# Banks of a score set on Trainium2: a third bank from anywhere, read by a second exponential, and a new rule string for the planner

## The chip, the cores and the metric

The kernel runs on one core of a Trainium2 chip. The metric is device time in microseconds (us) of one execution. The core's engines run side by side, each through its own list of instructions: TensorE (PE in the profile, its weight loads PEld), VectorE (DVE), ScalarE (ACT), GpSimd (POOL), and SyncE (SP), which issues most DMAs. PSUM, where TensorE writes, has eight banks of 512 fp32 columns by 128 partitions.

## The reference

One layer: attention with 32 query heads and one key and value head of width 20, beside a feed-forward block, both on the normalised input, added to it.

```python
xn = _layernorm(x)                        # x: 1 x 2048 x 640, bf16
q = (xn @ wq).reshape(B, S, 32, 20).transpose(0, 2, 1, 3)
k = xn @ wk                               # 2048 x 20
v = xn @ wv
p = softmax(einsum("bhqd,bkd->bhqk", q, k) * 20 ** -0.5)
o = einsum("bhqk,bkd->bhqd", p, v)
return x + o.transpose(0, 2, 1, 3).reshape(B, S, 640) @ wo + silu(xn @ w1) @ w2   # w1: 640 x 1728
```

## The kernel before

**The work.** Four blocks of 512 queries (QC) by eight groups of four heads (NG) make 32 groups; each has 16 tiles of 128 keys. One item is the scores of one head, one key tile and one block: a matmul of 32 rows by 128 columns of the array with 512 columns streamed (line 1078), into one PSUM bank. There are 32 x 16 x 4 = 2048 items. The four heads of a group lie on four row groups of the array, so up to four scores of different heads run side by side as one round.

**Two ways to the exponential.** An item is taken either by ScalarE, which reads two or three neighbouring banks with one Exp (line 1166) into slots of `Ebuf`, or by VectorE, which turns a whole batch of four items (one group, one key tile) into three integer approximations: a first step per item (line 1409, `p1`), then two shifts of the four together, on POOL (line 1448) or VectorE (line 1453). ScalarE takes key tiles from the front of a group, VectorE claims them from its back (`claim`). The products with V (line 1201) are column matmuls, four side by side as one round of 128 x 32 tiles, into the bank U of the group: one round for a key tile that ScalarE did, three for one that VectorE did. U is copied out by VectorE (line 1250), or added to what an earlier part left (line 1249).

**The other work** fills TensorE in between: projections to q (job "q"), the feed-forward's first product ("h", with a tanh on ScalarE at line 773 and its VectorE step at line 776), the second with the output projection ("out", VectorE at line 903), and for the last block "y" (line 919) and "fin" (line 967). These are column matmuls recorded by the helper `col_mm` (line 447); where a score run leaves a row group free, a slice of 32 rows can stand in it (`row_mm`, line 454). After each group its sums of weights go through DMAs and a reciprocal (lines 848 to 856) to POOL's product (line 860), and DMAs pack the result (line 873). If TensorE would have nothing to do for a while, a matmul of zeros is put in (`filler`, line 1725).

**What sets the order.** A planner, which runs on the host while the program is built, writes all five lists. It keeps a clock for each engine (`Sched`), always takes the engine whose clock is furthest back, and gives it the best of the operations at hand by a list of preferences. On TensorE these are: scores for ScalarE (`make_s_act`), scores for VectorE, products with V, and the other jobs. `plan(n)` picks the banks of ScalarE's n-th set from those that are free: the earliest three neighbouring banks if they come in time, else two. `act_until` says until when ScalarE has work, from its clock and the exponentials made but not begun. A set is made only when exponential n-2 has been committed.

The choices hang on some thirty numbers (`BASE`), and a letter stands for a variant of a few of them (`RULES`). `PLAN` is a string with one letter for each 10 us of the planner's TensorE clock; at each such step the numbers are set to `BASE` and the letter's variant. So a letter in the string changes the whole order from its place on. `split` and `spat`, which the change adds, are such numbers too.

Switching TensorE between row tiles (scores) and column tiles (the rest) costs a turn, so the planner gathers runs of each.

## Time and profile before

| | |
|---|---|
| median of 3 runs | 691.98 us (691.73 to 692.18) |
| the profiled execution | 691.7 us, its span 689.9 us |
| granted TensorE clock | 1.000 |
| instructions of the trace | 22614 |
| first exponential starts, last one ends | 13.35 us, 673.35 us |
| exponentials (line 1166) | 654: 590 of two banks, 64 of three |
| items by ScalarE / by VectorE | 1372 / 676 |
| matmul records at lines 1078, 1201, 447 | 2048, 3400, 3792 |

The profile's page gives busy time by engine, the span in 40 slices, the chain of work that ended last, and groups of instructions by line. In a row of a group stand the line, engine, operation, what is written and read, the shapes and the count; then the busy time in us and the mean duration in ns; then the idle time of the engine before these instructions, and what ended it. Timeline rows begin with the start and the length of a stretch in us. Rows of waits give the total in us, how often, and the longest. "Busy" counts a moment once however many instructions of the engine overlap in it.

The span has three parts: 13 us of loads and normalisation until the first exponential, the attention stage, and 16.6 us after the last exponential, in which the last groups' products and sums and the last output tiles are made.

### The profile page before, as it was taken

What the parts mean: (1) busy time and instruction counts of PE and PEld (TensorE: products, weight loads), DVE (VectorE), ACT (ScalarE), POOL (GpSimd) and SP (SyncE); (2) the same over time, 40 slices, a digit from 0 to 9 for tenths busy, and PEclk for the clock granted to TensorE, in tenths of its full rate; (3) what the DMA queues carried; (4) which work ended last, traced back from release to release, by engine and by line L of the source; (5) the groups of instructions that cost most, each with busy time, mean ns of one, the idle gap of its engine ahead of it and who ended that gap; (6) DMA issues with size and microseconds to landing.
All of it is one profiled execution on the core that took longest, in us unless ns stands there. A gap on an engine that the chain in (4) does not pass through costs nothing.

```text
span 689.9 us, 22614 instructions
## 1 busy us (share of the span) xinstructions
PE 676.4 (98%) x9870; PEld 234.4 (34%) x9873; DVE 594.7 (86%) x1017; ACT 665.9 (97%) x726; POOL 583.9 (85%) x351
## 2 busy tenths in 40 slices
PE   8999999999999999999999999999999999999998
PEld 5432222322233333323233333322232333333345
DVE  7899989988998867898988888798988889989973
ACT  6999999999999999999999999999999999999990
POOL 6668899898988889898899899989889998888860
PEclk9999999999999999999999999999999999999999
DMA  7753221122221232321212223222222202223201
GB/s 217 178 180 42 20 20 15 33 35 30 18 28 12 31 40 30 69 34 17 33 14 30 29 31 40 23 65 29 29 19 22 22 18 32 31 23 68 23 7 41
DMA packets 34241, 28.97 MB, mean 42 GB/s; under 512 B 15486, under 2 KB 29662, under 8 KB 34142
## 3 DMA queue, kind: packets, MB, share of 16 engines
q1 hardware_dynamic: 33854, 27.20, 25.7%
q8 instruction: 77, 1.26, 0.8%
q10 hardware_dynamic: 288, 0.33, 0.1%
q14 instruction: 22, 0.18, 0.1%
HBM read 11.09 MB, written 2.62 MB: 20 GB/s over the span
## 4 chain that ended last, share of the span: by engine, by line
PE 76%; ACT 16%; DVE 4%; POOL 1%; SPq 1%; DMA 1%; issue 1%; DVEq 0%; ACTq 0%
PE psall L1201 26%; PE psall L1078 25%; PE psall L447 23%; ACT sbt L1166 14%; DVE sbt L1409 1%; ACT sbt L773 1%; POOL sbt L1448 1%; SPq L706 1%; DMA sbt<-sbt 0%; PE psall L621 0%; DVE sbt L563 0%; PE psall L734 0%; DVE sbt L607 0%; PE psall L1725 0%; DVE sbt L565 0%
## 5 line engine op out<-in xcount | busy, mean ns | idle before, releaser
L1166 ACT ACTIVATE sbt<-psall 128x1024 bf16<-128x1024 f32 (+1 forms) x654 | 643.0, 1156 | 2.3 <-PE psall L1078 2.1
L1448 POOL TENSOR_SCALAR sbt<-sbt 128x2048 int16<-128x2048 int16 x275 | 521.7, 1897 | 70.4 <-DVE sbt L1453 22.4
L1409 DVE TENSOR_SCALAR sbt<-psall 128x512 int16<-128x512 f32 x676 | 441.8, 685 | 64.4 <-PE psall L1078 60.1
L1078 PE MATMUL psall<-sbt 32*128 32x512 bf16 x2048 | 269.2, 384 | 4.3 <-ACT sbt L1166 1.6
L1201 PE MATMUL psall<-sbt 128*32 128x512 bf16 x3400 | 264.8, 384 | 0.6 <-POOL sbt L1448 0.4
L447 PE MATMUL psall<-sbt 128*32 128x320 bf16 (+3 forms) x3792 | 227.6, 332 | 2.5 <-DVE sbt L1409 0.8
L1078 PEld LDWEIGHTS psall<-sbt 32*128 32x128 bf16 x2048 | 71.4, 91 | 238.8 <-ACT sbt L1166 172.7
L447 PEld LDWEIGHTS psall<-sbt 128*32 128x32 bf16 (+1 forms) x3792 | 82.4, 95 | 82.7 <-issue 44.7
L1201 PEld LDWEIGHTS psall<-sbt 128*32 128x32 bf16 x3400 | 70.1, 94 | 114.5 <-issue 71.0
L1453 DVE TENSOR_SCALAR sbt<-sbt 128x2048 int16<-128x2048 int16 x63 | 48.6, 784 | 0.7 <-PE psall L1201 0.6
L860 POOL TENSOR_TENSOR sbt<-sbt 128x512 bf16<-128x512 f32 x30 | 38.2, 1274 | 7.2 <-DVE sbt L1453 5.5
L776 DVE SCALAR_TENSOR_TENSOR sbt<-sbt,psall 128x512 bf16<-128x512 bf16 x52 | 35.6, 684 | 5.2 <-ACT sbt L773 2.6
L773 ACT ACTIVATE sbt<-psall 128x512 bf16<-128x512 f32 x52 | 37.6, 723 | 0.1
L1250 DVE COPY sbt<-psall 128x512 f32<-128x512 f32 x31 | 21.2, 683 | 1.1 <-PE psall L1201 1.0
L454 PE MATMUL psall<-sbt 32*128 32x320 bf16 x70 | 21.3, 305 | 0.0
L1725 PE MATMUL psall<-sbt 128*32 128x256 bf16 (+1 forms) x228 | 14.4, 355 | 1.2 <-DVE sbt L487 1.2
L693 DVE TENSOR_SCALAR sbt<-psall 128x512 bf16<-128x512 f32 x20 | 13.6, 680 | 0.4 <-PE psall L447 0.4
L903 DVE SCALAR_TENSOR_TENSOR sbt<-psall,sbt 128x320 bf16<-128x320 f32 x24 | 11.6, 485 | 2.1 <-PE psall L447 1.6
L572 POOL TENSOR_TENSOR sbt<-sbt 128x2 f32<-128x2 f32 x8 | 5.7, 709 | 8.7 <-DVE sbt L570 8.3
L585 POOL TENSOR_SCALAR sbt<-sbt 128x640 bf16<-128x640 bf16 x12 | 10.4, 874 | 1.5 <-DVE sbt L577 1.5
L919 DVE SCALAR_TENSOR_TENSOR sbt<-psall,sbt 128x320 f32<-128x320 f32 x8 | 3.9, 486 | 8.0 <-PE psall L447 8.0
L1725 PEld LDWEIGHTS psall<-sbt 128*32 128x32 bf16 x228 | 7.0, 114 | 4.5 <-issue 1.6
(64 smaller groups left out, 117.9 us busy)
## 6 DMA issues: line engine op xcount, KB each, us to landing
sbt<-sbt SPq DMA_DIRECT2D x120, 64.0 KB, 3.9
sbt<-in_A_x_dram SPq DMA_DIRECT2D x28, 160.0 KB, 4.0
sbt<-sbt SPq DMA_DIRECT2D x213, 20.0 KB
out_dram<-sbt SPq DMA_DIRECT2D x14, 160.0 KB, 2.0
sbt<-in_B_w_dram SPq DMA_DIRECT2D x1, 2160.0 KB, 13.4
sbt<-in_B_w_dram SPq DMA_DIRECT2D x1, 2080.0 KB, 8.1
sbt<-sbt SPq DMA_DIRECT2D x75, 8.0 KB
sbt<-in_A_wq_dram SPq DMA_DIRECT2D x1, 800.0 KB, 5.9
```

Of the source, the lines that this page charges most:

```text
L447: ins = pe.matmul(ps[j * SLOT:(j + 1) * SLOT, b * BANK + off:b * BANK + off + n], w[:, j * SLOT:(j + 1) * SLOT], x, start=start, stop=stop ...
L454: return pe.matmul(ps[0:w.shape[-1], b * BANK:b * BANK + n], w[k], x[k], start=start, stop=stop, tile_position=(r * SLOT, 0))
L773: t = Op("act", lambda a: a.activation(t_buf[0:rows, ts, :], bk(job.bank, 0, QW, rows=rows), AF.Tanh, scale=0.5), t_act(512), ACT_END, pre ...
L776: u = Op("dve", lambda v: v.scalar_tensor_tensor(out=hT[par][0:rows, fk, :], in0=t_buf[0:rows, ts, :], scalar=1.0, in1=bk(job.bank, 0, QW, ...
L860: nm = pool(lambda e: e.tensor_tensor(oU[:, us, :], U_sb[:, us, :], Rrep, ALU.mult), 1356.0, POOL_END, pre=[uc] + lc + pack_op.get(divmod( ...
L1078: return pe.matmul(bk(b), kT_rep[i * SLOT:(i + 1) * SLOT, kt * P:(kt + 1) * P], qT[i * SLOT:(i + 1) * SLOT, g % NQ, :], start=True, stop=T ...
L1166: return a.activation(Ebuf[:, es * QW:es * QW + w], ps[:, buf[0] * BANK:buf[0] * BANK + w], AF.Exp, scale=ESCALE)
L1201: ins = pe.matmul(ps[i * SLOT:(i + 1) * SLOT, ub * BANK:ub * BANK + QW], lhsT, rhs, start=(first and k < HG), stop=(last and k >= len(lst) ...
L1409: p1 = Op("dve", lambda v: v.tensor_scalar(z16[:, i * QW:(i + 1) * QW], bk(job.bank), ZBIAS, 0.0, ALU.add, ALU.max), t_dve(QW) + 2.0, DVE_ ...
L1448: op = pool(lambda v, t=t, j=j, zin=zin: v.tensor_scalar(t.bitcast(I16), zin, float(SHIFT[j]), 1.0, ALU.add, ALU.mult), POOL_SHIFT, POOL_E ...
L1453: op = dve(lambda v, t=t, j=j, zin=zin: v.tensor_scalar_add(t.bitcast(I16), zin, float(SHIFT[j])), t_dve(N, 4), prio=SPRIO - 0.01 * j, **args)
L1725: ins = pe.matmul(ps[i * SLOT:(i + 1) * SLOT, ub * BANK:ub * BANK + n], zero_t[:, 0:SLOT], zero_t[:, 0:n], start=fresh, stop=fresh, tile_p ...
```

## The change

A set for ScalarE is now a list of runs of neighbouring banks instead of one run. `plan` may return two neighbouring banks and one bank elsewhere (when `split` is 1 or 2), or three neighbouring banks as two and one (`split` 2); then `com` makes two exponentials, of two banks and of one, with successive numbers, and each frees its own banks. `exp_of` is the old body of `com` that makes one exponential. `act_until` looks back over four exponentials instead of two. Four letters are added, R, S, T and U, and `PLAN` is another string: it has the letters R, S and T at seven of its places. `split` is 0 under all other letters.

```diff
-BASE = dict(uopen=4, umin=3, ...)
+BASE = dict(split=0, spat=0.0, uopen=4, umin=3, ...)
...
+             R=dict(split=1), S=dict(split=2), T=dict(split=1, slack=500.0), U=dict(split=2, hungry=2000.0), ...
-PLAN = "acbtJKazNvhaJvxvixrrnrKzDDnQDmoqvknpfLBGvDPmoJdftFQdkttaQBBoknQEaoz"
+PLAN = "aaatJKazNvhaJvxoRozLfTDtJwDTQroaEBzSQaBkBkJvBvzQQttcrcBoTGSEaaatHBzR"
...
     def act_until(n):
-        return sc.t["act"] + sum(exp_ops[i].occ for i in (n - 2, n - 1) if i >= 0 and not exp_ops[i].done)
+        return sc.t["act"] + sum(exp_ops[i].occ for i in range(max(0, n - 4), n) if not exp_ops[i].done)
...
+            c2 = c if k == 2 else c2
         if w[3] is not None and (w[3][0] <= need + ru.patience or w[2][0] >= w[3][0]):
             s, r = w[3]
             if sc.t["dve"] < s + ru.dwant and not any(at[b] <= s + 40.0 for b in at if b not in r) and dve_items() is not None:
-                return r[:2]
-            return r
+                return [r[:2]]
+            return [r[:2], r[2:]] if ru.split >= 2 else [r]
+        if ru.split in (1, 2) and w[2] is not None:
+            c = [(max(s, at[b]), r, b) for s, r in c2 for b in at if b not in r]
+            if c:
+                s, r, b = min(c, key=lambda x: (x[0], -left_over(at, x[1] + (x[2],))))
+                if s <= need + ru.spat and not (sc.t["dve"] < s + ru.dwant and not any(at[x] <= s + 40.0 for x in at if x not in r and x != b) and dve_items() is not None):
+                    return [r, (b,)]
         if w[2] is None or w[2][0] < need - ru.hold:
             return None
-        return w[2][1]
+        return [w[2][1]]
...
+    def exp_of(s_op, n, run, es):
+        k = len(run)
+        for q in range(es, es + k):
+            e_owner[q] = n
+        eo = act(lambda a: a.activation(Ebuf[:, es * QW:(es + k) * QW], ps[:, run[0] * BANK:(run[0] + k) * BANK], AF.Exp, scale=ESCALE),
+                 t_act(k * QW) - 1.0, pre=[s_op], reads=[sc.banks[b] for b in run], writes=[res("E", es + q) for q in range(k)], prio=0.0, name=f"exp{n}")
+        eo.on_commit = lambda op: sc.free.update(run)
+        exp_ops[n] = eo
+        e_users[n] = []
...
-            eo = act(ef, t_act(w) - 1.0, pre=[op], reads=[sc.banks[b] for b in buf], writes=[res("E", es + k) for k in range(len(buf))], prio=0.0,
-                     name=f"exp{n}")
-            eo.on_commit = lambda op: sc.free.update(buf)
+            for run in runs:
+                exp_of(op, n, run, es + at)
+                for j in range(at, at + len(run)):
+                    mine[j] = n
+                at += len(run)
+                n += 1
+                att["n"] += 1
             for j, (g, kt, i) in enumerate(items):
                 d = pv_pend.setdefault((g, kt), {})
-                d[i] = (es + j, eo, n)
+                d[i] = (es + j, exp_ops[mine[j]], mine[j])
```

In the changed kernel the lines behind the new function lie ten further down (1201 is 1211, 1409 is 1419), and the exponential is line 1138.

More of the change, by code (lines that the diff above doesn't have):

```diff
@@ L103 @@
 TRACT = (0, 1)
-BASE = dict(uopen=4, umin=3, uleft=3, uwait=500.0, pace=-1.0, lagl=3, half=6, hold2=0, bnd=4, pj=6000.0, rows=0, rowmin=3, lagmax=6, lagp=0, lagj=6, openlag=5, late=-0.02, lead=0.01, leadmax=0.02, need=640.0, hold=300.0, dwant=600.0, slack=700.0, dnow=400.0, hungry=0.0, patience=0.0, keep=460.0, open=2, zcap=9, stay=0.0, homes=1, want=1, claim=6)
+BASE = dict(split=0, spat=0.0, uopen=4, umin=3, uleft=3, uwait=500.0, pace=-1.0, lagl=3, half=6, hold2=0, bnd=4, pj=6000.0, rows=0, rowmin=3, lagmax=6, lagp=0, lagj=6, openlag=5, late=-0.02, lead=0.01, leadmax=0.02, need=640.0, hold=300.0, dwant=600.0, slack=700.0, dnow=400.0, hungry=0.0, patience=0.0, keep=460.0, open=2, zcap=9, stay=0.0, homes=1, want=1, claim=6)
@@ L109 @@
-PLAN = "acbtJKazNvhaJvxvixrrnrKzDDnQDmoqvknpfLBGvDPmoJdftFQdkttaQBBoknQEaoz"
+             m=dict(need=740.0), n=dict(hold=0.0), o=dict(stay=640.0), p=dict(open=1), q=dict(slack=560.0), r=dict(hungry=1000.0), s=dict(claim=9), t=dict(open=3), u=dict(claim=4), v=dict(want=2), w=dict(slack=850.0), x=dict(hold2=4), y=dict(bnd=0), z=dict(pj=-1e9), A=dict(rows=0), B=dict(rows=2, rowmin=2), C=dict(pj=2000.0), D=dict(openlag=3), E=dict(pj=8000.0), F=dict(hold2=3), G=dict(rows=1), H=dict(half=0), I=dict(half=3), J=dict(stay=560.0), K=dict(stay=720.0), P=dict(need=560.0), Q=dict(hold=120.0), R=dict(split=1), S=dict(split=2), T=dict(split=1, slack=500.0), U=dict(split=2, hungry=2000.0), L=dict(uopen=3), M=dict(uopen=4), N=dict(uopen=5), O=dict(uopen=0))
@@ L1129, in make_s_act @@
             return None
-        buf = plan(n)
-        if buf is None:
+        runs = plan(n)
+        if runs is None:
             return None
+        buf = tuple(b for r in runs for b in r)
         items = next_items(len(buf), peek=True)
@@ L1136, in make_s_act @@
         buf = buf[:len(items)]
+        runs = [x for x in (tuple(b for b in r if b in buf) for r in runs) if x]
         pre = s_pre(items)
@@ L1182, in com @@
                         e_users[nn] = [o for o in e_users[nn] if o is not None] + [po]
-                else:
-                    pass
             for j, (g, kt, i) in enumerate(items):
-                d = pv_pend[(g, kt)]
-                if len(d) < HG and None not in e_users[n]:
-                    e_users[n].append(None)
+                if len(pv_pend[(g, kt)]) < HG and None not in e_users[mine[j]]:
+                    e_users[mine[j]].append(None)
             att["items"] += len(items)
```

19 lines of the change are left out of this document (4 added, 15 removed).

## The prediction

> **What bounds the kernel now.** I read the page's busy line first, then the groups by line and shape, then the stage between the first and the last exponential by itself, and last the timeline of ScalarE and TensorE inside it.
>
> ```profile
> PE 676.4 (98%) x9870; PEld 234.4 (34%) x9873; DVE 594.7 (86%) x1017; ACT 665.9 (97%) x726; POOL 583.9 (85%) x351
> ```
>
> ```profile
> L1166 ACT ACTIVATE sbt<-psall 128x1024 bf16<-128x1024 f32 x590 | 563.9, 1118 | 2.3 <-PE psall L1078 2.1
> L1166 ACT ACTIVATE sbt<-psall 128x1536 bf16<-128x1536 f32 x64 | 95.1, 1509 | 0.0
> L773 ACT ACTIVATE sbt<-psall 128x512 bf16<-128x512 f32 x52 | 37.6, 723 | 0.1
> L631 ACT ACTIVATE sbt<-psall 128x512 bf16<-128x512 f32 x3 | 2.0, 650 | 0.0
> ```
>
> ```profile
> 13.35:673.35 660.00, 652.44 (x9323) 216.54 (x9326) 578.73 (x973) 657.58 (x713) 575.67 (x328) 1.00 0.26 39
> ```
>
> The last row is the attention stage, 660.0 of the 689.9 us; its columns are length, then busy time (count) of PE, PEld, DVE, ACT and POOL, then clock. ScalarE (ACT) looks full, 657.58 us, and so does TensorE (PE), 652.44. Both are too high, because instructions overlap. The pitch, start to start, is what one really costs, and the timeline has it:
>
> ```profile
> 326.20 0.66 ACT L773 ACTIVATE sbt<-psall 128x512 bf16<-128x512 f32 x1
> 326.68 4.77 ACT L1166 ACTIVATE sbt<-psall 128x1024 bf16<-128x1024 f32 x5
> 331.19 0.74 ACT L773 ACTIVATE sbt<-psall 128x512 bf16<-128x512 f32 x1
> ```
>
> ```profile
> 664.06 9.52 ACT L1166 ACTIVATE sbt<-psall 128x1536 bf16<-128x1536 f32 x7
> ```
>
> ```profile
> 668.07 4.17 ACT L1166 ACTIVATE sbt<-psall 128x1536 bf16<-128x1536 f32 x3
> ```
>
> One bank (512) takes 326.68 - 326.20 = 0.48 us, two banks (331.19 - 326.68) / 5 = 0.902. The seven three-bank ones begin at 664.06 and the fifth to seventh, taken alone, begin at 668.07: (668.07 - 664.06) / 3 = 1.337. The smallest pitches of the trace are 0.477, 0.903 and 1.330. So a bank costs 0.427 us and every instruction 0.050 on top. Charged at these, ScalarE's stage is 590 x 0.903 + 64 x 1.330 + 57 x 0.477 (52 tanh, 2 more of line 744 and 3 of line 631) + 0.16 for one small copy = 645.5 us. Against the 660.0 that leaves **14.5 us of waits**, most of them hidden in pitches over the smallest. ScalarE is 97.8% loaded.
>
> TensorE the same way, where a run is a stretch of matmuls of one tile shape:
>
> ```profile
> 304.20 0.39 PE L1078 MATMUL psall<-sbt 32*128 32x512 bf16 x3
> 304.52 0.83 PE L447 MATMUL psall<-sbt 128*32 128x512 bf16 x12
> 305.29 0.39 PE L1078 MATMUL psall<-sbt 32*128 32x512 bf16 x3
> 305.61 0.62 PE L447 MATMUL psall<-sbt 128*32 128x512 bf16 x8
> 306.16 0.39 PE L1078 MATMUL psall<-sbt 32*128 32x512 bf16 x3
> ```
>
> ```profile
> 674.48 2.89 PE L447 MATMUL psall<-sbt 128*32 128x320 bf16 x80
> 677.29 1.05 PE L999 MATMUL psall<-sbt 128*128 128x4 f32 x8
> ```
>
> Twelve column matmuls (three rounds of four) take 0.77 us, eight take 0.55: 0.216 a round and 0.115 for the turn to the next shape. A run of scores takes 0.32: one round and 0.104 for its turn, whether it holds two, three or four. Rounds 320 wide cost (2.81 - 0.10) / 20 = 0.136. Summed over the program's 649 score runs, 643 column runs and 28 others this is 650.1 us, 628.2 of it from the first score to the last, or 95% of the stage. So ScalarE is the tighter of the two, TensorE the next, and VectorE (578.73 of 660, 88%) only follows:
>
> ```profile
> PEld psall L1078 <- ACT sbt L1166: 172.7, 479, 0.8
> DVE sbt L1409 <- PE psall L1078: 60.1, 170, 1.4
> ```
>
> Scores wait 479 times for a bank that an exponential leaves, which is the sign of ScalarE as the bound, and VectorE waits for scores.
>
> By the Trainium skill, "Perfetto Trace Analysis", section Identifying the Most-Contended Engine, matmul occupancy is no measure of the distance from the limit and the weight loads' share is to be taken instead, while ScalarE's occupancy may stand. The page's 34% for PEld agrees that 98% is not TensorE at its limit.
>
> **The change, part by part.** Both kernels' orders are fixed when they are built, so the instructions can be counted in both.
>
> *The planner's code.* The older planner's steps are unchanged while `split` is 0. The sum over four older exponentials instead of two adds nothing then, since exponential n-2 must be committed before a set is made. An exponential that reads neighbouring banks is the same instruction. I charge this nothing: it is work of the host.
>
> *The order.* It is the same on ScalarE up to about 154 us of charged work, and another one from there on. Only eight sets are split in the whole program (at about 154, 205, 262, 264, 340, 341, 568 and 572 us of ScalarE's charged work); a ninth one-bank exponential is the leftover at the end. So the two-and-one set does little by itself: three-bank scores were 64 and are 55 + 8 = 63. What moves time is the new string.
>
> *ScalarE.* Two-bank exponentials go from 590 to 601, three-bank from 64 to 55, one-bank from 0 to 9: 665 for 654, and 1376 banks for 1372. Sum: 11 x 0.903 - 9 x 1.330 + 9 x 0.477 = **+2.3 us**, of it 4 banks x 0.427 = 1.7 and 11 x 0.050 = 0.55. No cover hides this: it is on the tightest engine, unless its 14.5 us of waits shrink.
>
> The Trainium skill, "ScalarE: Activation LUTs", section What ACT_TABLE_LOAD costs, gives 186 ns and 0.833 ns an element, less about 93 ns where two follow each other, so 93 ns for each further instruction where the pitches above give 50. By it the sum would be 4 x 0.427 + 11 x 0.093 = 2.7 us, an estimate; it speaks against splitting.
>
> *VectorE and GpSimd (POOL).*
>
> ```profile
> L1409 DVE TENSOR_SCALAR sbt<-psall 128x512 int16<-128x512 f32 x676 | 441.8, 685 | 64.4 <-PE psall L1078 60.1
> L1453 DVE TENSOR_SCALAR sbt<-sbt 128x2048 int16<-128x2048 int16 x63 | 48.6, 784 | 0.7 <-PE psall L1201 0.6
> L1249 DVE TENSOR_TENSOR sbt<-psall,sbt 128x512 f32<-128x512 f32 x6 | 4.1, 682 | 0.0
> L1448 POOL TENSOR_SCALAR sbt<-sbt 128x2048 int16<-128x2048 int16 x275 | 521.7, 1897 | 70.4 <-DVE sbt L1453 22.4 <-PE psall L1201 16.1 <-DVE sbt L1409 6.2
> ```
>
> First steps 676 to 672, shifts 63 to 62, partial sums of U 6 to 9: -4 x 0.653 - 0.77 + 3 x 0.68 = -1.3 us. POOL has one shift less, -1.9. Both have slack, so by itself this is worth nothing.
>
> *TensorE.* One batch less on VectorE turns three products with V into one: 3400 matmuls become 3392. Fills of 512 columns go from 16 to 13 and those of 256 from 41 to 42, ten more slices of the other products slip into score runs, and runs go to 650, 645 and 27. By the pitches above the sum is 649.1, **-1.0 us**. A fill is issued where the planner sees a hole on TensorE: three holes fewer.
>
> *DMAs.*
>
> ```profile
> PE 76%; ACT 16%; DVE 4%; POOL 1%; SPq 1%; DMA 1%; issue 1%; DVEq 0%; ACTq 0%
> ```
>
> ```profile
> 375.63 3.41 DMA sbt<-sbt
> ```
>
> The same transfers stand in another order on SP's queue. DMAs are 1% of the chain of work that ended last, and the longest piece there took 3.41 us; that one percent is what hides them at present, so I charge nothing. If one came late, a job of products would be held back, by 3.4 us at most.
>
> *What the waits become.* This is the disputed term: the trace of before cannot show it. Bounds: ScalarE's waits stay at 14.5 us (the sum is +2.3), or they fall by what the other engines' progress tells. That can be counted: put both orders side by side at equal charged work of ScalarE, and ask what the others have been given by then.
>
> | ScalarE's charged work, us | scores issued, before / after | TensorE's charged work, before / after |
> |---|---|---|
> | 370 | 1137 / 1131 | 363.0 / 359.7 |
> | 470 | 1458 / 1453 | 459.6 / 456.8 |
> | 570 | 1785 / 1777 | 558.3 / 554.5 |
> | 620 | 1953 / 1947 | 607.5 / 604.2 |
> | 649 | 2042 / 2037 | 633.7 / 631.9 |
>
> From 370 on TensorE has done 3.0 us less and VectorE some six scores less (ScalarE's own count is equal within one). If TensorE stays as full as it was (95.4%), 3.0 / 0.954 = 3.1 us less have passed; if VectorE keeps its rate, 6 x 0.653 / 0.877 = 4.5 us less. ScalarE would then have waited 3.1 to 4.5 us less, and with its 2.3 us more work the sum is -0.9 to -2.2. I take the middle, **-1.5 us**, because fewer fills say that TensorE's holes did not grow. After the last score both programs have 13.4 us of TensorE work left, so the tail adds nothing.
>
> The profiled execution took 691.7 us (its span of 689.9 and 1.8 around it), so the sum is 691.7 - 1.5 = 690.2 for it. The median of the runs, 691.98, lies 0.28 higher; on its scale the forecast is 690.4 after rounding down from 690.5.
>
> **The rivals.**
>
> *The added load counts in full; slower.* ScalarE's 11 further exponentials and four further banks, from 154 us of charged work to the end, cost 2.3 us, and the other engines' smaller progress is simply idleness: their scores wait longer for banks. For it: ScalarE is the tightest, its visible idle before exponentials is 2.3 us only, and three-bank sets, the cheapest per bank, are nine fewer. I also charged TensorE against ScalarE over stretches of four exponentials: what TensorE has in excess adds up to 9.9 us in both orders, so the new one is no smoother. Against: three fills fewer. It decides from the point where ScalarE's waits stay above 12.2 us. Time 691.98 + 2.3 = 694.3. [...]
>
> *The changes cancel; within 0.2%.* ScalarE +2.3, TensorE -1.0, VectorE -1.3: three engines that wait for each other in turn, each keeping its idle time on the average, give a sum of zero. Eight split sets in 665 then show nothing. Time 692.0.
>
> *The split saves a whole run at each place.* Had each of the eight sets saved a score run (0.32 us) ahead of a starved ScalarE, that would be 2.6 us beside the forecast, 690.4 - 2.6 = 687.8. Against: the number of score runs rises by one.
>
> **How the numbers follow.** A measurement of this kernel can tell about 0.2%, 1.38 us: faster is below 690.6, slower above 693.4. Chances: forecast 0.40 and the saved runs 0.02, which together are faster, 0.42; cancelling 0.25; full load 0.33. The forecast is the likeliest. Since cases of both signs hold much of the chance, its own range is 688.6 to 691.2; the range of all reaches from 688.6, where ScalarE's waits have fallen by 5.7 us (the 4.5 of VectorE's reading and four of the eight saved runs, 1.3), to 694.4, the full load; a late DMA and the whole split saving are left out.
>
> **What would show it.** Right: ScalarE's charged work is 647.7 us in the stage, its waits 10 to 12, the stage some 1.5 us shorter, the tail unchanged. Wrong: the waits stay near 14.5 and scores wait as long or longer for exponentials; or new waits stand at the eight one-bank exponentials; or a DMA appears in the chain of waits. The stage until 154 us of charged work should be the same within 0.2 us.

## The result, and the profile after

The changed kernel takes 695.1 us in the median of four executions, the kernel before 691.9 beside it: ratio 1.0049, 95% interval [1.0037, 1.0061]. Two of the four ran at a granted clock of 1.000 (694.4 and 694.5 us) and two at 0.997 (695.7 and 696.0). Five further executions, all at 0.999 or 1.000, gave 694.6 and a ratio of 1.0039 [1.0027, 1.0052] (experiment e5). I therefore take the change as **+2.8 us**; where a difference of 1 us matters below, I compare medians of executions at 0.999 or more. The forecast was 690.4, range 688.6 to 694.4: wrong in its sign, and the result lies above the range.

The page of the changed kernel, its span and first and fourth part:

```profile
span 692.5 us, 22605 instructions
...
PE 677.0 (98%) x9855; PEld 235.9 (34%) x9855; DVE 589.3 (85%) x1015; ACT 667.3 (96%) x737; POOL 582.8 (84%) x350
...
ACT 63%; PE 34%; DVE 1%; POOL 1%; DMA 0%; issue 0%; POOLq 0%; ACTq 0%
```

The busy line has hardly moved. The chain of work that ended last has: 76% TensorE and 16% ScalarE before, 63% ScalarE and 34% TensorE now. It is tempting to read from this which engine to make lighter. Experiments e13 to e16 show that it doesn't say that.

Groups by line and shape, ScalarE's exponentials and VectorE's first steps:

```profile
L1138 ACT ACTIVATE sbt<-psall 128x1024 bf16<-128x1024 f32 x601 | 577.5, 1124 | 2.8 <-PE psall L1078 2.7
...
L1138 ACT ACTIVATE sbt<-psall 128x1536 bf16<-128x1536 f32 x55 | 84.0, 1565 | 0.0
...
L1419 DVE TENSOR_SCALAR sbt<-psall 128x512 int16<-128x512 f32 x672 | 439.3, 684 | 71.4 <-PE psall L1078 66.5 <-PE psall L454 0.4
...
L1138 ACT ACTIVATE sbt<-psall 128x512 bf16<-128x512 f32 x9 | 6.4, 710 | 0.0
```

The counts are those that the prediction took from the order: 601, 55 and 9. VectorE waits longer for scores, 66.5 us for 60.1.

Charged at the prediction's pitches, the span of each profiled execution falls into the start (first exponential at 13.6 us), ScalarE's work, its waits, and the rest after the last exponential. (The table of the time before has the first exponential at 13.35 us and the end of the last at 673.35. The trace has 13.59 and 673.59; the stage is 660.0 us long either way. Here the last exponential is charged at its pitch, so the rest begins 0.2 us before it ends.)

| | ScalarE's work, us | its waits | after the last exponential | span | last score starts | from there to the end |
|---|---|---|---|---|---|---|
| before | 645.3 | 14.5 | 16.5 | 689.9 | 671.05 | 18.86 |
| after | 647.6 | 13.9 | 17.4 | 692.5 | 673.02 | 19.50 |
| difference | +2.3 | -0.6 | +0.9 | +2.6 | +1.97 | +0.64 |

The waits were to fall by 3.1 to 4.5 us and fell by 0.6. By stage (to 165, 300, 450, 620 us, and the rest) they were 4.3, 3.0, 2.9, 3.5 and 0.9, and are 4.1, 2.6, 2.2, 4.2 and 0.8. At equal charged work of ScalarE, counted from the first exponential, the changed kernel is 1.3 us ahead at 400 us of work and 0.2 us at 520. So the waits fell at first, by less than half of the forecast, and most of it came back between about 425 and 545 us of the span.

**Where TensorE lost time.** The windows of the stages, columns as in the prediction; before:

```profile
165.00:300.00 135.00, 133.72 (x1951) 44.13 (x1943) 114.68 (x186) 134.74 (x143) 119.04 (x66) 1.00 0.23 31
300.00:450.00 150.00, 148.75 (x2201) 49.60 (x2202) 129.16 (x212) 149.85 (x161) 135.52 (x75) 1.00 0.25 30
450.00:620.00 170.00, 168.48 (x2415) 54.20 (x2412) 152.31 (x250) 169.73 (x186) 151.59 (x86) 1.00 0.23 28
```

and after:

```profile
165.00:300.00 135.00, 134.03 (x1995) 45.43 (x1987) 112.05 (x183) 134.69 (x146) 122.14 (x67) 1.00 0.23 32
300.00:450.00 150.00, 146.23 (x2139) 48.74 (x2140) 125.47 (x206) 150.00 (x161) 136.26 (x76) 1.00 0.24 27
450.00:620.00 170.00, 168.20 (x2384) 54.99 (x2376) 151.50 (x251) 169.16 (x189) 146.12 (x83) 1.00 0.24 32
```

From 300 to 450 us TensorE's busy time falls by 2.5 us and VectorE's by 3.7, while ScalarE is busy all the time. In the stage ahead of it the new order had run 44 matmuls more (1995 for 1951). The groups of 300 to 450 us say which ones are missing later. Before:

```profile
L1201 PE MATMUL psall<-sbt 128*32 128x512 bf16 x792 | 61.0, 384 | 0.0
L1078 PE MATMUL psall<-sbt 32*128 32x512 bf16 x473 | 60.9, 384 | 0.4 <-ACT sbt L1166 0.2
...
L447 PE MATMUL psall<-sbt 128*32 128x512 bf16 x328 | 26.4, 384 | 0.4 <-DVE sbt L1409 0.2 <-DVE sbt L776 0.2
...
L1725 PE MATMUL psall<-sbt 128*32 128x512 bf16 x4 | 0.4, 379 | 0.0
L1725 PE MATMUL psall<-sbt 128*32 128x256 bf16 x4 | 0.3, 272 | 0.0
```

After:

```profile
L1211 PE MATMUL psall<-sbt 128*32 128x512 bf16 x792 | 61.6, 384 | 1.8 <-DVE sbt L1419 0.6 <-POOL sbt L1458 0.5 <-DVE sbt L1260 0.5
L1078 PE MATMUL psall<-sbt 32*128 32x512 bf16 x474 | 61.4, 384 | 1.5 <-ACT sbt L1138 1.2 <-DVE sbt L1419 0.3
...
L447 PE MATMUL psall<-sbt 128*32 128x512 bf16 x256 | 20.1, 383 | 0.1
...
L1735 PE MATMUL psall<-sbt 128*32 128x512 bf16 x16 | 1.4, 382 | 0.0
```

Scores and products with V are as many as before. Of the other products, those of 512 columns (to q and the feed-forward's first, which wait for no exponential) are 256 for 328; in the stage ahead they had been 260 for 200. Those of 320 columns are about as many (576 for 572). Now TensorE is idle ahead of products with V (1.8 us for 0.0) and of scores (1.5 for 0.4). The waits of the same window, before:

```profile
DVE sbt L1409 <- PE psall L1078: 18.3, 53, 1.2
...
PEld psall L1078 <- DVE sbt L1409: 2.3, 6, 0.4
...
PEld psall L1201 <- DVE sbt L1409: 1.4, 5, 0.4
```

and after:

```profile
DVE sbt L1419 <- PE psall L1078: 21.5, 48, 2.1
...
PEld psall L1078 <- DVE sbt L1419: 5.9, 15, 0.5
...
PEld psall L1211 <- DVE sbt L1419: 2.9, 8, 0.5
```

VectorE waits longer for scores, and TensorE's weight loads wait longer for VectorE. The longest hole, from the timeline of all engines:

```profile
370.56 1.05 PE L1211 MATMUL psall<-sbt 128*32 128x512 bf16 x16
...
371.54 0.39 PE L1078 MATMUL psall<-sbt 32*128 32x512 bf16 x3
371.66 0.69 DVE L1260 COPY sbt<-psall 128x512 f32<-128x512 f32 x1 [0.26 <-PE psall L1211]
...
372.26 2.48 DVE L1419 TENSOR_SCALAR sbt<-psall 128x512 int16<-128x512 f32 x4
...
372.32 0.47 PE L1078 MATMUL psall<-sbt 32*128 32x512 bf16 x4 [0.40 <-ACT sbt L1138]
...
373.24 0.39 PE L1078 MATMUL psall<-sbt 32*128 32x512 bf16 x3 [0.45 <-ACT sbt L1138]
...
373.60 0.10 PEld L1211 LDWEIGHTS psall<-sbt 128*32 128x32 bf16 x4 [0.27 <-DVE sbt L1419]
373.60 0.40 PE L1211 MATMUL psall<-sbt 128*32 128x512 bf16 x4
```

Three sets of scores stand one behind the other, with nothing between them. TensorE waits for a bank, issues four scores, waits again, and then waits for a first step, which VectorE began only after copying U of the group that ended. Ten scores take 2.06 us (371.54 to 373.60), of which three rounds and a turn, 0.75, are work. Such excess over the charged pitches adds up, from 300 to 450 us, to 5.5 us before and 8.9 after; in the stages to either side it changes by -0.8 (165 to 300) and +0.6 (450 to 620).

This says where TensorE stood idle, not yet what that cost. ScalarE itself waited 0.7 us less in this stage (2.9 to 2.2) and 0.7 more in the next (3.5 to 4.2). By which wait the lost time reaches the end is not shown.

**The tail.** TensorE's last runs, before:

```profile
671.04 0.39 PE L1078 MATMUL psall<-sbt 32*128 32x512 bf16 x3
...
678.28 1.08 PE L1017 MATMUL psall<-sbt 128*32 128x128 f32 x32
679.18 7.42 PE L447 MATMUL psall<-sbt 128*32 128x320 bf16 x212
```

and after:

```profile
673.01 0.39 PE L1078 MATMUL psall<-sbt 32*128 32x512 bf16 x3
...
677.71 1.95 PE L1017 MATMUL psall<-sbt 128*32 128x128 f32 x64
679.48 9.73 PE L447 MATMUL psall<-sbt 128*32 128x320 bf16 x280
```

After the last score stand twice as many of the fp32 matmuls of line 1017 (64 for 32, 0.028 us each: (679.48 - 677.71) / 64) and a longer last run, which starts 0.30 us later and lasts 2.3 longer. From the last score to the end it is 0.64 us more, and it is 0.6 to 0.7 more in every pair of the two orders below that was made lighter or heavier.

### The profile page after: what moved, and what is told of

Read it like the earlier page. It is cut to its first block, busy times and chain, and to the rows that moved or that the text cites. A ratio compares the mean times of both kernels' runs of the same rounds, so it can differ in the third digit from the quotient of the medians.

```text
span 692.5 us, 22605 instructions
## 1 busy us (share of the span) xinstructions
PE 677.0 (98%) x9855; PEld 235.9 (34%) x9855; DVE 589.3 (85%) x1015; ACT 667.3 (96%) x737; POOL 582.8 (84%) x350
## 3 DMA queue, kind: packets, MB, share of 16 engines
q1 hardware_dynamic: 33854, 27.20, 25.3%
## 4 chain that ended last, share of the span: by engine, by line
ACT 63%; PE 34%; DVE 1%; POOL 1%; DMA 0%; issue 0%; POOLq 0%; ACTq 0%
ACT sbt L1138 58%; PE psall L1211 11%; PE psall L1078 11%; PE psall L447 10%; ACT sbt L773 3%; POOL sbt L1458 1%; PE psall L595 1%; PE psall L621 1%; DMA sbt<-in_A_x_dram 0%; DVE sbt L1419 0%; PE psall L999 0%; PE psall L1017 0%; ACT sbt L554 0%; DVE sbt L565 0%; DVE sbt L563 0%
## 5 line engine op out<-in xcount | busy, mean ns | idle before, releaser
L1419 DVE TENSOR_SCALAR sbt<-psall 128x512 int16<-128x512 f32 x672 | 439.3, 684 | 71.4 <-PE psall L1078 66.5
L1211 PEld LDWEIGHTS psall<-sbt 128*32 128x32 bf16 x3392 | 69.4, 94 | 117.2 <-issue 76.0
L1463 DVE TENSOR_SCALAR sbt<-sbt 128x2048 int16<-128x2048 int16 x62 | 44.4, 730 | 0.1
L454 PE MATMUL psall<-sbt 32*128 32x320 bf16 (+1 forms) x80 | 24.7, 309 | 0.1
L1735 PE MATMUL psall<-sbt 128*32 128x256 bf16 (+1 forms) x220 | 12.4, 344 | 1.2 <-DVE sbt L487 1.2
L595 PE MATMUL psall<-sbt 128*128 128x128 bf16 x80 | 6.9, 220 | 1.5 <-DVE sbt L588 1.5
```

Of the source, the lines that this page charges most:

```text
L454: return pe.matmul(ps[0:w.shape[-1], b * BANK:b * BANK + n], w[k], x[k], start=start, stop=stop, tile_position=(r * SLOT, 0))
L1211: ins = pe.matmul(ps[i * SLOT:(i + 1) * SLOT, ub * BANK:ub * BANK + QW], lhsT, rhs, start=(first and k < HG), stop=(last and k >= len(lst) ...
L1419: p1 = Op("dve", lambda v: v.tensor_scalar(z16[:, i * QW:(i + 1) * QW], bk(job.bank), ZBIAS, 0.0, ALU.add, ALU.max), t_dve(QW) + 2.0, DVE_ ...
L1463: op = dve(lambda v, t=t, j=j, zin=zin: v.tensor_scalar_add(t.bitcast(I16), zin, float(SHIFT[j])), t_dve(N, 4), prio=SPRIO - 0.01 * j, **args)
```

## The experiments

Theories at the start. **Load**: ScalarE's 2.3 us of further work is the loss. **Wait**: ScalarE's waits take up added work, and the order of the others is what costs. From e6 on a third stands beside them, **both engines**: ScalarE and TensorE hold each other up, and what counts is the order. Later ones are named where they come in. In the table, "work" is the change of one engine's charged work against the kernel that the edit starts from, the time is the median of the executions at a clock of 0.999 or more, and the ratio is of all executions, lower clocks included. The kernels in which an engine is made lighter leave that part of the computation out.

| run | starts from | work, us | time, us | ratio to before, 95% |
|---|---|---|---|---|
| e1 | before | ScalarE +3.2 | 694.5 | 1.0040 [1.0028, 1.0052] |
| e2 | after | ScalarE -2.2 | 693.6 | 1.0031 [1.0019, 1.0043] |
| e3 | before | order of the end | 691.6 | 0.9998 [0.9989, 1.0006] |
| e4 | after | no set split | 702.7 | 1.0165 [1.0150, 1.0179] |
| e5 | after | none | 694.6 | 1.0039 [1.0027, 1.0052] |
| e6 | before | ScalarE -2.2 | 690.8 | 0.9987 [0.9979, 0.9996] |
| e7 | before | 56th letter E | 695.1 | 1.0048 [1.0034, 1.0061] |
| e8 | before | 54th letter B | 695.4 | 1.0055 [1.0041, 1.0068] |
| e9 | before | TensorE +3.5 | 693.9 | 1.0043 [1.0030, 1.0057] |
| e10 | after | TensorE +3.5 | 697.0 | 1.0085 [1.0071, 1.0099] |
| e11 | before | 44th letter S | 694.7 | 1.0044 [1.0031, 1.0057] |
| e12 | before | 44th letter a | 700.6 (clock 0.995 to 0.997) | 1.0127 [1.0113, 1.0141] |
| e13 | before | ScalarE -8.7 | 690.1 | 0.9986 [0.9977, 0.9996] |
| e14 | after | ScalarE -8.9 | 693.0 | 1.0029 [1.0017, 1.0041] |
| e15 | before | TensorE -7.3 | 690.0 | 0.9977 [0.9968, 0.9987] |
| e16 | after | TensorE -7.3 | 693.2 (one of four executions) | 1.0039 [1.0024, 1.0054] |
| e17 | before | VectorE -26 | 690.9 | 0.9988 [0.9979, 0.9997] |
| e18 | after | VectorE -26 | 693.7 | 1.0039 [1.0024, 1.0055] |

### What a further exponential costs (e1)

In the kernel before, each of the 64 three-bank exponentials is issued as one of two banks and one of one. Nothing else moves.

```diff
+                if len(buf) == 3:
+                    a.activation(Ebuf[:, es * QW:(es + 2) * QW], ps[:, buf[0] * BANK:(buf[0] + 2) * BANK], AF.Exp, scale=ESCALE)
+                    return a.activation(Ebuf[:, (es + 2) * QW:es * QW + w], ps[:, buf[2] * BANK:buf[2] * BANK + QW], AF.Exp, scale=ESCALE)
```

> The kernel before with its order kept, but each of the 64 three-bank exponentials issued as a two-bank and a one-bank exponential (what a split set looks like to ScalarE, on neighbouring banks). ScalarE's charged work rises by 64 x 0.050 = 3.2 us and nothing else changes. Load theory (ScalarE's work from the first to the last exponential passes to the end in full): +3.2 us, about 695.1. Wait theory (ScalarE's 14.5 us of waits take it up, and it is the order of the others that costs): within 0.7 us of before, 691.2 to 692.6.

The groups of e1; lines 1166 and 1167 are the two halves:

```profile
L1169 ACT ACTIVATE sbt<-psall 128x1024 bf16<-128x1024 f32 x590 | 566.7, 1149 | 2.0 <-PE psall L1078 1.9
...
L1166 ACT ACTIVATE sbt<-psall 128x1024 bf16<-128x1024 f32 x64 | 72.3, 1129 | 0.0
...
L1167 ACT ACTIVATE sbt<-psall 128x512 bf16<-128x512 f32 x64 | 45.5, 711 | 0.0
```

694.5 us, 2.8 more, of 3.2 charged: 0.044 us for each of 64 added instructions. The wait theory (at most 692.6) falls. So work added to ScalarE in an unchanged order costs nearly its full pitch, and the 11 further instructions of the change cost about 0.5 us. The Trainium skill, "ScalarE: Activation LUTs", section What ACT_TABLE_LOAD costs, with 93 ns for each further instruction, would make an estimated 6.0 us of the 64; the measurement is less than half of that, and it decides.

### Taking ScalarE's added work away (e2, e6), and the changed kernel again (e5)

In both kernels every exponential leaves out the last four columns of its last bank.

```diff
-        eo = act(lambda a: a.activation(Ebuf[:, es * QW:(es + k) * QW], ps[:, run[0] * BANK:(run[0] + k) * BANK], AF.Exp, scale=ESCALE),
+        eo = act(lambda a: a.activation(Ebuf[:, es * QW:(es + k) * QW - CUT], ps[:, run[0] * BANK:(run[0] + k) * BANK - CUT], AF.Exp, scale=ESCALE),
```

> The changed kernel with its order kept, each exponential reading and writing 4 columns fewer (the last 4 columns of each set's last bank are left out of the computation and hold a constant). ScalarE's work falls by 665 x 4 x 0.833 ns = 2.2 us, about what the change added. Load theory: 2.2 us less than the changed kernel's 694.4 at full clock, 692.2. Wait theory: 694.4, within 0.7.

> The kernel before with its order kept and each exponential 4 columns narrower (the last 4 columns of each set's last bank are left out and hold a constant): ScalarE's work falls by 654 x 4 x 0.833 ns = 2.2 us. Load theory: 691.8 - 2.2 = 689.6. In the changed kernel the same cut brought 0.5 us of span, its waits rose by 1.8. If TensorE binds in turn as soon as ScalarE gets shorter (both-engines theory): -0.5 to -1.0, about 691.0, with the waits of ScalarE risen by 1.2 to 1.7.

> The changed kernel once more, for its interval beside the other runs of this call. Load theory and wait theory alike: 694.4 where the granted clock is 1.000; two of its four runs had a clock of 0.997 and took 1.4 us longer, and if the order itself brings the lower clock on, it will show in about as many again.

With ScalarE's work equal to that of before (645.4 for 645.3 us), the changed kernel still takes 693.6, 1.9 us more than before; its waits rose from 13.9 to 15.7. The same edit on the kernel before brought 1.0 of 2.2, and there too the rest came back as waits (14.5 to 15.7). Two microseconds taken from ScalarE are worth one in either order: the load theory in its full form falls, since it gives at most 0.9 of the 2.8 by this measure.

### Shifting work between the stage and the tail (e3)

The kernel before with another 66th letter, which moves feed-forward products from the tail into the stage.

```diff
-PLAN = "acbtJKazNvhaJvxvixrrnrKzDDnQDmoqvknpfLBGvDPmoJdftFQdkttaQBBoknQEaoz"
+PLAN = "acbtJKazNvhaJvxvixrrnrKzDDnQDmoqvknpfLBGvDPmoJdftFQdkttaQBBoknQEahz"
```

> The kernel before with one letter near the end of its string changed (the 66th, to h): the order is the same until about 640 us, then ScalarE gets one batch of four banks more, as in the change (1376 banks; its work rises by 1.75 us), and less is left for TensorE after the last score (11.4 us by the pitches, for 13.9). Load theory with the tail counted by its TensorE work: 691.9 + 1.75 - 2.6 = 691.1. If the tail is a chain that can't get shorter: 693.6. If ScalarE's load is taken up by waits: 689.3.

The last score came 2.7 us later, the way from there to the end was 2.6 shorter (16.3 for 18.9), the time the same: 691.6. That is nearest to the account that counts the tail by its TensorE work (691.1). In this run work moved across the last score cost as much ahead of it as it saved behind it.

### The changed string without any split (e4)

```diff
-             R=dict(split=1), S=dict(split=2), T=dict(split=1, slack=500.0), U=dict(split=2, hungry=2000.0), ...
+             R={}, S={}, T=dict(slack=500.0), U=dict(hungry=2000.0), ...
```

> The changed kernel with its string, but with no letter allowing a split. The order is another one from the first split on; ScalarE's work rises by 11.5 us against the changed kernel (90 sets of three, 567 of two, 1404 banks), and the TensorE work after the last score falls from 14.3 to 5.4 us. Load theory: 694.4 + 11.5 - 8.9 = 697.0, or more if the tail is a chain with a floor. Wait theory: the time goes with the order's smoothness, not the load; nothing makes this one less smooth, so 693 to 696.

702.7, where the highest number named was 697.0 "or more": ScalarE's work is 659.1 and its waits 17.8, 3.9 more than after. From the last score to the end it took 11.9 us, though only some 5.4 us of TensorE's work stand there. So the string was made for the splits, or for the order that they bring; taken without them it is another order and a poor one. The run says nothing on what eight split sets are worth by themselves.

### Other letters: equal load, other order (e7, e8, e11, e12)

Each is the kernel before with one letter changed; e11 and e12 have the change's code, and at place 44 one has the splitting letter S, the other a plain a.

```diff
-PLAN = "acbtJKazNvhaJvxvixrrnrKzDDnQDmoqvknpfLBGvDPmoJdftFQdkttaQBBoknQEaoz"
+PLAN = "acbtJKazNvhaJvxvixrrnrKzDDnQDmoqvknpfLBGvDPmoJdftFQdkttEQBBoknQEaoz"
```

```diff
-PLAN = "acbtJKazNvhaJvxvixrrnrKzDDnQDmoqvknpfLBGvDPmoJdftFQdkttaQBBoknQEaoz"
+PLAN = "acbtJKazNvhaJvxvixrrnrKzDDnQDmoqvknpfLBGvDPmoJdftFQdkBtaQBBoknQEaoz"
```

```diff
-PLAN = "acbtJKazNvhaJvxvixrrnrKzDDnQDmoqvknpfLBGvDPmoJdftFQdkttaQBBoknQEaoz"
+PLAN = "acbtJKazNvhaJvxvixrrnrKzDDnQDmoqvknpfLBGvDPSoJdftFQdkttaQBBoknQEaoz"
```

```diff
-PLAN = "acbtJKazNvhaJvxvixrrnrKzDDnQDmoqvknpfLBGvDPmoJdftFQdkttaQBBoknQEaoz"
+PLAN = "acbtJKazNvhaJvxvixrrnrKzDDnQDmoqvknpfLBGvDPaoJdftFQdkttaQBBoknQEaoz"
```

> The kernel before with the 56th letter of its string changed to E: the same order until about 550 us; ScalarE's work falls by 1.9 us (1368 banks) and the TensorE work after the last score falls from 13.9 to 7.3 us, so that the stage before it holds 6.7 us more of TensorE's work (635.0 us by the pitches, for 628.2). Load theory with waits unchanged: -1.9 and up to -6.6 for the tail, 683 to 690. Both-engines theory (after about 550 us TensorE has no idle time left to take in 6.7 us): the last score comes later by what the tail loses, ScalarE's waits rise by 6 to 8 us, and the time is 691 to 693.

> The kernel before with the 54th letter changed to B: the same counts on ScalarE (590 and 64, work unchanged), 6.9 us less TensorE work after the last score, 7.4 us more before it. Load theory with waits unchanged: up to 6.9 us faster, 685 to 690. Both-engines theory: ScalarE's waits rise by as much as the tail gets shorter, 691 to 693.

> The changed planner with before's string but its 44th letter S (a set may be split, nothing else): the same order until about 430 us. Two split sets; ScalarE's work +0.2 us on before's, TensorE's work +0.4 us in all and 2.0 us of it moved from the tail into the stage. Both-engines theory: time within 1.5 us of before, 691 to 693.5; if a split set saves a whole score run in front of a starved ScalarE, below 691.

> As the run with the letter S, but with the letter a in its place: the same numbers in the planner's rules, without the split. ScalarE's work +5.2 us on before's (609 + 46 banks become 1384), 8.5 us of TensorE's work moved from the tail into the stage, TensorE's whole work +0.6 us. Both-engines theory: more idle time on TensorE, 694 to 699; what the letter S is better by is what the split brings at this place, with all that follows from it.

e8 has exactly the exponentials of before (645.3 us of work) and a tail 6.6 us shorter (12.26), and takes 3.6 us more: its waits are 24.0 us. e7 has 1.9 us less of ScalarE's work and 6.2 less of tail, and takes 3.3 more: waits 25.3. The load theory (at most 690) missed both by over 5 us. "Both engines" (at most 693) had the rise of the waits right and missed by 2.1 and 2.4. The load of the fullest engine ranks these orders wrongly.

e11 has the load of before (645.5) with two split sets and 3.0 us more (waits 18.3), above what "both engines" gave it (693.5). e12 has none and about 9 more, above its 699; in its trace the granted clock is 0.5 for 6.8 us (538.8 to 545.7), so an estimated 3 of these come from the clock, at 1.4 us for 3.4 us of it (see the last section). (Its expectation has a slip: 609 + 46 exponentials aren't 1384 banks. The trace has 584 of two and 72 of three, which are.) At one place S is then some 3 us better than a at equal clock, with all that follows from the letter. A letter's worth isn't the worth of the sets that it splits.

### Adding work to TensorE (e9, e10)

Sixteen rounds of products with zeros (64 matmuls, 16 x 0.216 = 3.5 us) are put ahead of products with V, spread over scores 930 to 1360, which is where the changed kernel's holes are.

```diff
+            if flags.get("extra"):
+                for i in range(HG):
+                    pe.matmul(ps[i * SLOT:(i + 1) * SLOT, flags["bank"] * BANK:flags["bank"] * BANK + QW], zero_t[:, 0:SLOT], zero_t[:, 0:QW],
+                              start=False, stop=False, tile_position=(0, i * SLOT))
```

> The kernel before with its order kept and 16 extra rounds of four matmuls of zeros (16 x 0.216 = 3.5 us of TensorE) ahead of 16 products with V, spread over the stretch in which the scores 930 to 1360 of 2048 are issued, about 300 to 440 us. They add zeros to U, so the output stays. Both-engines theory (here TensorE has no more idle time than it needs between its runs): most of it passes to the end, +1.7 to +3.5 us, 693.5 to 695.3. Load theory (ScalarE alone sets the pace): under 0.7 us.

> The same 16 rounds in the changed kernel, over the same scores. Its trace has 3.4 us more of TensorE's idle time between 300 and 450 us than before's. Hole theory (that time is a usable reserve which the new string wastes): at most +1.2 us on 694.4, so under 695.6, and clearly less than what the same rounds cost before. If the idle time is no reserve, as much as before: 696 to 698.

Groups of e9, the added ones and the products with V:

```profile
L1202 PE MATMUL psall<-sbt 128*32 128x512 bf16 x3400 | 266.3, 384 | 0.6 <-POOL sbt L1456 0.4
...
L1215 PE MATMUL psall<-sbt 128*32 128x512 bf16 x64 | 6.3, 383 | 0.0
```

+2.25 us on the kernel before (693.89 - 691.64), +2.5 on the changed one ((696.96 - 691.64) - 2.8). A third theory said that the holes of 300 to 450 us are idle time which further work would fill for nothing. It fails at the sixteen places tried: the kernel with more idle time on TensorE pays as much. None of the sixteen fell into the long hole, though. In e10's trace the ten scores take the same 2.06 us (373.10 to 375.16), and the zeros beside them run at 366.3 and 376.1 us. Whether work placed inside the hole would be free was not tried.

The Trainium skill, "Perfetto Trace Analysis", section Identifying the Most-Contended Engine, would have TensorE's distance from its limit judged by its share of the peak arithmetic and by the busy share of its weight loads. The second is 34% here, which taken alone would mean room. The runs don't bear that out for this kernel: 3.5 us of added matmuls cost two thirds of themselves.

### Making one engine lighter in both kernels (e13 to e18)

If the difference came from one engine's load or durations, it should shrink when that engine has slack in both kernels. Exponentials 16 columns narrower (e13, e14: CUT = 16 in the edit of e2); 320-wide products 32 columns narrower (e15, e16); 396 of VectorE's 676 first steps (392 of 672 in the changed kernel) 64 columns narrower (e17, e18):

```diff
+                if n == HALF:
+                    fn = n, w, x = n - LESS, w, x[..., 0:n - LESS]
```

```diff
-        p1 = Op("dve", lambda v: v.tensor_scalar(z16[:, i * QW:(i + 1) * QW], bk(job.bank), ZBIAS, 0.0, ALU.add, ALU.max),
+        less = LESS if zi < NZ else 0
+        p1 = Op("dve", lambda v: v.tensor_scalar(z16[:, i * QW:(i + 1) * QW - less], bk(job.bank, 0, QW - less), ZBIAS, 0.0, ALU.add, ALU.max),
```

> The kernel before, order kept, each exponential 16 columns narrower (the last 16 columns of each set's last bank are left out and hold a constant): ScalarE's work falls by 654 x 16 x 0.833 ns = 8.7 us. With 4 columns less 2.2 us of load brought 1.0 us. If TensorE now binds: 1 to 3 us faster than before, 689 to 691. If ScalarE went on to set the pace: 683.

> The same in the changed kernel, ScalarE 8.9 us lighter. Load account (the difference of the two kernels is ScalarE's 2.3 us): with ScalarE light in both the difference to the run before goes to zero or below, since TensorE has 1.0 us less work here. Order account (the new order holds TensorE up by itself): 1.5 us or more over the run before.

> The kernel before, order kept, the products of 320 columns narrower by 32 (the last 32 columns of each half of an output row are left out): TensorE's work falls by 552 rounds x 13.3 ns = 7.3 us, most of it after 200 us and 2 us in the tail. Both-engines theory: 2 us in the tail and about half of the rest, 687 to 689. Load theory: the tail's 2 us alone, 689.7.

> The same in the changed kernel (two rounds fewer of 320 columns, the tail has ten more of them). Load account: with TensorE light in both kernels ScalarE's 2.3 us pass in full, so 2.0 to 2.5 us over the run before. Order account: the difference falls to 1 us or less, since the new order's holds on TensorE have room now.

> The kernel before, order kept, 396 of VectorE's 676 first steps narrower by 64 of 512 columns (these columns are left out and hold a constant): 67 ns earlier each, 26 us of VectorE's work less. Load account: VectorE is busy 88% and only follows, no change, 691.2 to 691.8. VectorE account: its waits on TensorE's side are 1.4 us for products with V and 3.4 for the other products, a part of which goes: 0.3 to 1.5 us faster.

> The same in the changed kernel (392 of 672 first steps). VectorE account: 4.3 us of TensorE's holes stand behind first steps ahead of products with V, 44 of them, so up to 67 ns x 44 = 2.9 us more can go; it gains at least 0.8 us more than the kernel before does, and the difference of the two falls from 2.8 to 2.0 or less. Order account without VectorE: both gain alike, the difference stays at 2.6 to 3.0.

| pair | changed kernel's time less that of before, each against the kernel before that ran beside it, us |
|---|---|
| as they are (e5) | 2.8 |
| ScalarE 2.2 lighter (e2, e6) | 2.9 |
| ScalarE 8.8 lighter (e13, e14) | 3.0 |
| TensorE 7.3 lighter (e15, e16) | 3.2 |
| VectorE 26 lighter (e17, e18) | 2.8 |
| TensorE 3.5 heavier (e9, e10) | 3.1 |

Each ratio has an interval of 0.1 to 0.15% to either side (0.6 to 1.1 us), so these do not differ; the value for TensorE rests on one full-clock execution of e16. The ScalarE pair leaves its difference of 2.3 us in place, but makes it cheap: from 2.2 to 8.7 us off, the kernel before gained only 0.5 more (1.0 to 1.5), so 2.3 us of ScalarE's work there are worth an estimated 0.2 (2.3 x 0.5 / 6.5), and the difference is still 3.0.

Of the expectations, e14 came out as its order account had it (1.5 or more), and e18 as the account without VectorE (2.6 to 3.0). In e16 the order account failed in its own terms: the difference was to fall to 1 us or less, and it is 3.2, nearer to the load account (2.0 to 2.5). e15 was to come to 687 to 689 by "both engines" and came to 690.0, near the load theory's 689.7; but that theory had the tail 2 us shorter, and it is 0.5 (18.36 for 18.86).

Against the kernel before beside each, ScalarE made 8.7 to 8.9 us lighter brought 1.5 us in the old order and 1.3 in the new (2.8 - 1.5); TensorE made 7.3 lighter brought 1.6 and 1.1 (2.8 - 1.7). The chain's shares, 76% and 16% before, 34% and 63% after, told in neither kernel which engine to make lighter.

The window of 300 to 450 us in e13:

```profile
300.00:450.00 150.00, 149.09 (x2206) 49.70 (x2204) 129.29 (x212) 149.28 (x162) 135.97 (x75) 1.00 0.26 32
```

and in e14:

```profile
300.00:450.00 150.00, 146.78 (x2128) 48.42 (x2128) 124.56 (x204) 148.94 (x161) 135.91 (x75) 0.99 0.24 27
```

With ScalarE 8.8 us lighter in both, TensorE is again 2.3 us and VectorE 4.7 us less busy here in the changed order. TensorE's excess in this stage is 5.1 and 9.6 us (e13, e14), 7.0 and 10.7 (e15, e16), 5.7 and 9.9 (e17, e18), beside 5.5 and 8.9. Of the 9.6 and 9.9 some 1.3 to 1.4 us are the runs of matmuls in a stretch at half clock, which e14's and e18's traces have in this stage (last section), so the rise is some 3 us in these two pairs, 3.7 in the third and 3.4 without an edit. The hole near 371 us is 1.3 us long in the changed kernel, in e14 and in e18. So the loss goes with the order: making ScalarE, TensorE or VectorE lighter, one at a time, doesn't remove it. Making several lighter at once was not tried.

## Why the prediction was wrong, point by point

- **Where both orders are the same** (to 154 us of charged work): right; ScalarE's waits to 165 us are 4.3 and 4.1 us.
- **ScalarE +2.3 us**: right as work (645.3 to 647.6; the recorded sum for before, 645.5, comes to 645.2 from its own terms, and the stretch at 668.07 from which a pitch was read starts with the fourth exponential of the seven, not the fifth, so that 1.337 is right). As a price it was too simple: by e2 it is worth 0.9 us in the changed order, by e1's rate (2.8 of 3.2) at most 2.0.
- **TensorE -1.0, VectorE -1.3, planner's code and DMAs nothing**: the DMAs were right (0% of the chain). Smaller work on these two engines was to be worth something only through the waits. It is worth little: e15 and e17 took off 7.3 and 26 us for 1.6 and 0.8.
- **The 479 waits as "the sign of ScalarE as the bound"** said too much. They are waits of weight loads. The matmul side of TensorE stood idle for an exponential ahead of scores only 1.6 us, in five places, and 8.7 us off ScalarE brought 1.5.
- **"What the waits become" is the step that failed.** The waits were to fall by 3.1 to 4.5 us and fell by 0.6. The step counted how far behind TensorE and VectorE were at equal work of ScalarE and turned this into time saved, "if TensorE stays as full as it was (95.4%)". It didn't stay so: in part TensorE was behind because it stood idle, its excess from 300 to 450 us going from 5.5 to 8.9 us. ScalarE's gain at equal work reached 1.3 us at 400 us of work and was 0.2 at 520. The same table could be read either way, and the rival did read it as "idleness". The reason for choosing, "fewer fills say that TensorE's holes did not grow", was poor evidence: in this very stage the matmuls of zeros (line 1725, after 1735) rose from 8 to 16. The new order had run more of the products of 512 columns from 165 to 300 us (260 for 200), and from 300 to 450 it had fewer to put between scores (256 for 328).
- **"The tail adds nothing"**: mis-sized. The charged 13.4 us were to be equal; the counts given with e3 and e4 have 13.9 before and 14.3 after. From the last score to the end the chip took 0.64 us more, with 32 fp32 matmuls more of 0.028 us each (0.9 us) among it.
- **"The split saves a whole run"** fell, as the count of runs had said. **"The changes cancel"** fell.
- **The full-load rival** (694.3) came within 0.3 us of the 694.6, but not by its mechanism. The identity +2.3 - 0.6 + 0.9 puts all of it on the load, while e2 shows that 1.9 of the 2.8 stay when the load is equalised, and e13 with e14 that all of it stays when ScalarE has slack. A sum that comes out right isn't a cause; to come so near was luck.
- **The range** ended at the full load, 694.4, as if waits could only shrink. The orders e7, e8, e11 and e12 show that a change of order moves ScalarE's waits by 4 to 11 us, and in these four always upward.

**What stays open.** Which dependency of the new order makes the holes: the scarcity of ready products, the rotation of banks, or the change of group with its copy of U. The trace shows all three meeting near 371 us; I have argued from it that the products spent early are what is missing, but no run put them back. Whether TensorE's idle time from 300 to 450 us brings on ScalarE's waits after 450, and how, is open too. The two-and-one set by itself was not shown to gain or lose: eight sets are too few to measure, and by e1 they cost at most 0.5 us. No long wait stands at them: ScalarE's three longest between 165 and 660 us (0.62, 0.59 and 0.44 us) are at 257.5, 542.4 and 549.6 us, and the eight one-bank exponentials between 166.8 and 592.7, none within 15 us of these. No version that beats the kernel before came out of these runs; e13, e15 and e17 are quicker because they leave work out.

## What to carry to other kernels

Where several engines are nearly full in a fixed order (84 to 98% busy here), a sum of loads did not forecast a new order: measure what a microsecond added to and taken from each engine is worth, and expect the two to differ. "This engine has done less by then" is only good news if it wasn't waiting, so look at what it still has to run in each stage before turning lag into time saved. Test a claim about load by lightening that engine in both versions: if the difference stays, that engine's load is not its cause.

## What the hardware showed

- Adding and taking away are not priced alike. ScalarE: 3.2 us added cost 2.8 (e1); 2.2 taken off brought 1.0 (e6), and 8.7 only 1.5 (e13). TensorE: 3.5 added cost 2.25 (e9), 7.3 taken off brought 1.6 (e15). VectorE: 26 taken off brought 0.8 (e17).
- The granted clock of one core was not the same in all executions of a program. Of the changed kernel's nine, two ran at 0.997 and took about 1.4 us more; e12's four all ran at 0.995 to 0.997. In the traces the loss is one stretch at a granted clock of 0.50, with 1.00 around it: 3.4 us in e14 (373.6 to 377.0 us) and in e18 (375.1 to 378.6), 6.8 us in e12. In the first two it stands right behind the long hole near 371 us; the changed kernel and e5 have the same hole without it, so that one brings the other is not shown.
- The lower clock goes with the order. Below 0.999 were 13 of 36 executions of the changed order (the changed kernel, e2, e5, e10, e14, e16, e18) and 4 of 131 of the order before (the kernel before beside e1 to e18, e1, e6, e9, e13, e15, e17). The 2.8 us leave this out, so over all executions the change costs somewhat more.
